# Transposing half of the query tiles on VectorE instead of TensorE, and moving statistics and side sums to other engines, in a fused adaLN block

## The chip, the cores and the metric

The kernel runs on one core of a Trainium2 chip. A core has five engines that each work through a queue of their own, in order, and wait for each other by semaphores: TensorE (PE in the profile, its weight loads PEld), VectorE (DVE), ScalarE (ACT), GpSimd (POOL) and SyncE (SP), which here does nothing but issue DMA transfers. The metric is the device time of one execution in microseconds (us), lower is better.

## The reference

`x` is 2048 tokens of 512 features. Six vectors of modulation come from `silu(c) @ w_mod`. Then, in float32:

```
h = layernorm(x) * (1 + ca) + sa
q, k, v = h @ wqkv                       # 32 heads of 16 features
pq, pk = phi(q), phi(k)                  # phi(t) = (t > 0 ? t + 1 : exp(t)) + 1e-6
o = (pq @ (pk^T v)) / (pq . sum(pk) + 1e-6)        # linear attention, per head
x = x + ga * (o @ wo)
h = layernorm(x) * (1 + cb) + sb
x = x + gb * (((h @ w_gate) * (h @ w_up)) @ w_down)  # 1376 hidden features
```

## The kernel before

The tokens are cut into 16 tiles of 128, four tiles to a chunk (chunks 0 to 3). Float32 products are made of three TensorE products in the type float32r: each operand is split into a high half (a rounded copy, made by ScalarE) and a low half (what is left, made by VectorE or GpSimd), and high x high, high x low and low x high are added up in PSUM (`split` L195, `product` L205).

A first stage computes keys, values and their per-head products for all tiles. From them and `wo` it folds one matrix `wp` per 128 features (`w_out` L596), so that the attention's output of a token tile is its normalised query features times `wp`. The query tiles `phq[i]` are held with tokens in the partitions; `den_a` (L573), `den_b` (L579) and `den_c` (L583) compute each head's denominator and divide by it on VectorE.

The second stage, which the change touches, goes tile by tile. TensorE needs the query tile with features in the partitions, so `turn_a` (L655) transposes it in four 128x128 blocks on TensorE into a PSUM bank; `turn_h` (L661) makes the high half on ScalarE and `turn_l` (L665) the low half on VectorE, both reading the bank. `y_seed` (L680) copies the residual `x` into an accumulator bank on ScalarE, `y_a` (L688) adds the 12 products with `wp` on TensorE, and `y_b` (L697) copies the sum y back to `x` on ScalarE and takes the statistics of the second layer norm on VectorE (`Norm.stats` L225: `bn_stats`, `bn_aggr`). `y_step(i)` (L703) strings this together: transposes of tile i+1, products of tile i, halves of tile i+1, `y_b` of tile i-1, seed of tile i+1. When a chunk's four tiles are done, `rstd_of`, `nmr_of` and `xhat` (L231 to L247) normalise it: VectorE, then one GpSimd power, then VectorE, then four ScalarE passes.

Between the steps of this stage TensorE is fed other work: the last query projections, and, for chunks 0 and 1, the products of three of the eleven blocks of hidden features (`gate_up` L765, `down` L786), whose results VectorE evicts (`evac` L755). The modulated second-norm features of chunks 0 and 1 are also stored to DRAM (`kept`) and loaded back for the last stage. Chunks 2 and 3 are turned for that stage without TensorE: `stow` (L815) writes a tile to DRAM with its 32-row groups regrouped, `unstow` loads it, and `flip` (L827) transposes its 32x32 blocks on VectorE.

The last stage (`ffn` L1091) does the remaining feed-forward products for pairs of chunks, in a form that needs sums and differences of the left operands (`Left.sum` L872: s1 to s4 for two halves, `first[0]` and `first[1]`) and of the right operands (`Right.sums`, `Right.high`, `Right.lows`, L926 to L952).

The order is written out by hand: nothing is reordered, so every engine runs its instructions in the order of the program text from L1136 on. All tiles in SBUF come from one pool of 94 buffers; a new tile takes a free buffer and its first writer waits for that buffer's last readers. All transfers are issued from SP's queue, in order; a transfer that waits holds back those behind it.

Of the kernel before, what the change touches and what calls it, by code (L numbers as in the profile page):

```python
# [24 lines left out]
def tile_adaln_block(  # L25
# [39 lines left out]
    small = pool("small", 2)  # L65
    tiles = pool("tiles", NB)
# [3 lines left out]
    def f32(ap):  # L70
        return ap.bitcast(F32)
# [3 lines left out]
    def T(p, tag, shape=(P, D), dt=F32, bufs=None):  # L75
        cnt[0] += 1
        return p.tile(list(shape), dt, tag="t" if p is tiles else tag, name=f"{tag}_{cnt[0]}", bufs=bufs)

    def B(tag, shape=(P, D), dt=F32):

        return T(tiles, tag, shape, dt)

    def acc_bank():
        return T(ps_acc, "acc")
# [128 lines left out]
    def cut(pair, a, b):  # L213
        return pair[0][:, a:b], pair[1][:, a:b]


    class Norm:
        def __init__(self, tiles):
            self.tiles = tiles
            self.mv = T(small, "mv", (P, NJ, 2))  # L220
            self.n = [None] * NJ
            self.ps = [None] * KD
            self.t = [None] * KD

        def stats(self, *js, of=None):  # L225
            for j in js:
                st = T(small, "st", (P, 6), bufs=4)
                nc.vector.bn_stats(st, self.tiles[j] if of is None else of)
                nc.vector.bn_aggr(self.mv[:, j], st)

        def rstd_of(self, a=0, b=NJ):  # L231
            if a == 0:
                self.rstd = T(small, "rstd", (P, NJ))
                self.nmr = T(small, "nmr", (P, NJ))
                self.ve = T(small, "ve", (P, NJ))
            nc.vector.tensor_scalar(self.ve[:, a:b], self.mv[:, a:b, 1], EPS_LN, None, op0=ALU.add)  # L236
            nc.gpsimd.tensor_tensor(self.rstd[:, a:b], self.ve[:, a:b], half[:, a:b], op=ALU.pow)  # L237

        def nmr_of(self, a=0, b=NJ):
            nc.vector.scalar_tensor_tensor(self.nmr[:, a:b], self.mv[:, a:b, 0], -1.0, self.rstd[:, a:b],  # L240
                                           op0=ALU.mult, op1=ALU.mult)

        def xhat(self, *js):
            for j in js:
# [41 lines left out]
    NT = NCH * NJ  # L286
    norm = [Norm(xts[0])]
    wk, wq, wv = [], [], []
    kx, phk, phq, q_ps = {}, {}, {}, {}
# [169 lines left out]
    rows, cols = {}, {}  # L459
# [113 lines left out]
    def den_a(ch, *js, on=None):  # L573

        for j in js:
            den_p(ch, j, on=on)
            den_r(ch, j)

    def den_b(ch):  # L579
        nc.vector.tensor_tensor(dens[ch], dens[ch], den0.unsqueeze(1).to_broadcast([P, NJ, NH]), op=ALU.add)  # L580
        nc.vector.reciprocal(dens[ch], dens[ch])

    def den_c(*tiles):  # L583

        for i in tiles:
            ch, j = divmod(i, NJ)
            p3 = phq[i].rearrange("p (h i) -> p h i", i=DH)
            nc.vector.scalar_tensor_tensor(p3, p3, EPS_PHI, dens[ch][:, j].unsqueeze(2).to_broadcast([P, NH, DH]),
                                           op0=ALU.add, op1=ALU.mult)
# [65 lines left out]
    def turn_a(i):  # L655
        tps[i] = turn_bank[0]()
        phi = phq.pop(i)
        for k in range(KD):
            nc.tensor.transpose(tps[i][:, k * P:(k + 1) * P], phi[:, k * P:(k + 1) * P], ident)

    def turn_h(i):  # L661
        pqs[i] = (B("xh", dt=F32R), B("xl", dt=F32R))
        nc.scalar.activation(pqs[i][0], tps[i], AF.Copy)

    def turn_l(i):  # L665
        h, l = pqs[i]
        nc.vector.tensor_tensor(l, tps.pop(i), f32(h), op=ALU.subtract)

    def turn(i):
        turn_a(i)  # L670
        turn_h(i)
        turn_l(i)

    y_banks = []

    def y_bank():
# [3 lines left out]
    def y_seed(i, of=acc_bank):  # L680

        yps[i] = of()
        if of is bank:

            nc.tensor.matmul(yps[i], wp[0][0][:, :P], wp[0][0], start=True, stop=True)
        nc.scalar.activation(yps[i], xts[i // NJ][i % NJ], AF.Copy)

    def y_a(i):  # L688
        if i not in yps:
            y_seed(i)  # L690
        pq = pqs.pop(i)
        for k in range(KD):
            (ah, al), (bh, bl) = cut(pq, k * P, (k + 1) * P), wp[k]
            for x, y in ((ah, bh), (ah, bl), (al, bh)):
                nc.tensor.matmul(yps[i], x, y, start=False, stop=k == KD - 1 and x is al, skip_group_check=True)  # L695

    def y_b(i):  # L697
        ch, j = divmod(i, NJ)
        ps = yps.pop(i)
        nc.scalar.activation(xts[ch][j], ps, AF.Copy)  # L700
        norm2[ch].stats(j, of=ps)

    def y_step(i, *more, late=(), q=None, turn=True, seed=acc_bank):  # L703

        if q is not None:
            ps = proj(q, wq)
        if turn and i + 1 < NT and i + 1 not in pqs:
            turn_a(i + 1)
        y_a(i)
        if i + 1 in tps:  # L710
            turn_h(i + 1)
            turn_l(i + 1)
        if i - 1 in yps:
            y_b(i - 1)
        if q is not None:
            q_a(q, ps)
        if seed and i + 1 < NT:
            y_seed(i + 1, seed)
        for do in more:
            do()  # L720
        for do in late:
            do()
# [14 lines left out]
    def scale_down(f):  # L737
        d = raw_f[f][2]
        nc.vector.tensor_tensor(d, d, gb[:d.shape[0]], op=ALU.mult)
# [46 lines left out]
    def down(ch, js=range(NJ), ahead={}, parts=(lone,)):  # L786

        dn = {j: acc_bank() for j in js}
        for step, (part, j) in enumerate((part, j) for part in parts for j in js):
            for do in ahead.get(step, ()):  # L790
                do()
            a, b = j * P, (j + 1) * P
            for f in part:
                n = fts[f][1]
                (hh, hl), (dh, dl) = hs[ch, f], wf[f][2]
                nc.tensor.matmul(dn[j], hh[:n, a:b], dh[:n], start=f == lone[0], stop=False)
                nc.tensor.matmul(dn[j], hh[:n, a:b], dl[:n], start=False, stop=False)
                nc.tensor.matmul(dn[j], hl[:n, a:b], dh[:n], start=False, stop=f == lone[-1])
        return lambda: evac(ch, dn, js)
# [15 lines left out]
    def stow(ch, *js):  # L815

        for j in js:
            to = stowed[ch, j] = tc.dram_tile([P, D], F32, name=f"stowed_{ch}_{j}")
            to = to.rearrange("(q i) (m c) -> m i q c", i=BL, c=P)
            for m in range(NQ):  # L820
                nc.sync.dma_start(to[m], norm2[ch].n[j][m * BL:(m + 1) * BL].rearrange("i (q c) -> i q c", c=P))
# [37 lines left out]
    class Left:  # L859
# [9 lines left out]
                c, k = self.of[n]  # L869
                self.f[n] = load(kept[c][k], "f") if c in PLAIN else blocks.pop((c, "f", k))  # L870

        def sum(self, *names):  # L872
            for n in names:
                x, y, alu = {"s1": ("a21", "a22", ALU.add), "s3": ("a11", "a21", ALU.subtract),
                             "s2": ("s1", "a11", ALU.subtract), "s4": ("a12", "s2", ALU.subtract)}[n]
                self.f[n] = B("s")
                nc.vector.tensor_tensor(self.f[n], self.f[x], self.f[y], op=alu)

        def split(self, *names, low=None):
            for n in names:  # L880
# [265 lines left out]
    y_step(0, lambda: den_c(3), lambda: q_b(11))  # L1146
    y_step(1)
    y_step(2, lambda: split_gu(f0, nc.gpsimd))
    y_step(3, lambda: scale_down(f0), turn=False, seed=False)
    ps12 = proj(12, wq)  # L1150
    y_b(3)
    norm2[0].rstd_of()
# [36 lines left out]
    den_c(7)  # L1189
    den_a(2, 2, on=nc.vector)  # L1190
    g()
    y_step(5)
    y_step(6, lambda: den_a(2, 3, on=nc.vector))
    y_step(7, turn=False, seed=False)
    y_b(7)
    norm2[1].rstd_of()
    den_b(2)
    ln2_nx(1)
    den_c(8)
    take = down(0, ahead={3: (lambda: turn(8), lambda: y_seed(8, bank), lambda: den_c(9, 10))})  # L1200
    take()
    ln2_turn(1, 0, 1)
    y_step(8)
    ln2_turn(1, 2, 3)
    y_step(9)
    side.update(plain_side((0, 1)))
    first = [Left((0, 1), k).into(side) for k in range(KH)]
    for x in first:
# [2 lines left out]
    right_load(1)  # L1211
    g = gate_up(1, f0)
    den_a(3, 0, 1, on=nc.vector)
    den_c(11)
    g()
    y_step(10)
    g = gate_up(1, f1)
    den_a(3, 2, 3, on=nc.vector)
    g()
    y_step(11, turn=False, seed=False)  # L1220
    y_b(11)
    norm2[2].rstd_of()
    den_b(3)
    g = gate_up(1, f2)
    den_c(12)
    norm2[2].nmr_of()
    norm2[2].xhat(0, 1)
    first[0].sum("s1", "s3")
    g()
    norm2[2].xhat(2, 3)  # L1230
    stow(2, 0, 1, 2, 3)
    turn_a(12)
    take = down(1, (0, 1), parts=((f0, f1), (f2,)))
    den_c(13)
    turn_h(12)
    turn_l(12)
    y_banks += [acc_bank(), acc_bank()]
    y_seed(12, y_bank)
    first[0].sum("s2", "s4")
    take()  # L1240
    den_c(14)
    y_step(12, seed=y_bank)
    take = down(1, (2, 3))
    first[1].sum("s1", "s3", "s2", "s4")
    first[0].split("s1", "s2")
    take()
    den_c(15)
    y_step(13, seed=y_bank)
    right_sums(0, nc.vector)
    for n in range(4):  # L1250
        banks.append(bank())
# [88 lines left out]
```

## Time and profile before

| | |
|---|---|
| median of 3 runs | 561.06 us (560.93 to 561.57) |
| the profiled execution | 560.93 us, span of its trace 559.2 us |
| granted TensorE clock | 0.999 |
| statistics of y, VectorE L228 | 690 ns each |
| transposes of query tiles, TensorE L659 | 64 |
| DMA, all of the span | 52.01 MB, 29.1% of the 16 engines |

The span is what the trace covers; the time of the execution is 1.7 us longer. A row of a group gives line, engine, operation, output <- input, shape, count, then busy time in us and mean ns of one, then the idle time of the engine before them and what ended it. In the chain that ended last each row is a start, a length and the work that held the end up at that moment. In a row of a table by stage stand the stage, then for PE, PEld, DVE, ACT and POOL the busy us with the count of instructions, then the granted clock, the DMA share and GB/s.

### The profile page before, as it was taken

To read this page: it belongs to the slowest core of one execution; us is meant where nothing else is said; L and a number is where in the kernel's file an instruction comes from. 1 tells how busy PE (TensorE), PEld (TensorE's weight loads), DVE (VectorE), ACT (ScalarE), POOL (GpSimd) and SP (SyncE) were. 2 spreads that over 40 slices of the span, in tenths; PEclk is the share of its full clock that TensorE was granted. 3 is DMA by queue.
4 is the path that set the end of the run, shared out by engine and by line. 5 is a ranking of instruction groups with operands and counts; after the bars stand their busy time and mean duration, and the time that the engine had idled before them with its cause. 6 is when DMAs were issued, how large, how long until landed. Compare 5 with 4: busy or idle time off the path is not lost.

```text
span 559.2 us, 7301 instructions
## 1 busy us (share of the span) xinstructions
PE 552.8 (99%) x2539; PEld 453.4 (81%) x2539; DVE 383.7 (69%) x629; ACT 281.0 (50%) x503; POOL 190.1 (34%) x195
## 2 busy tenths in 40 slices
PE   8999999999999999999999999999999999999997
PEld 6788888888888778878887888877888888888886
DVE  7896968968969876859877697796543544344435
ACT  3695866546557546344883445554343333333110
POOL 2000000100011300001599666566667446446200
PEclk9999999999999999999999999999999999999999
DMA  8900212210501000814425152591335222200004
GB/s 289 385 4 2 75 55 96 93 60 3 154 2 74 2 1 38 264 33 119 132 59 149 58 192 71 175 321 36 114 113 151 56 57 57 58 19 1 1 0 151
DMA packets 51077, 52.01 MB, mean 93 GB/s; under 512 B 7712, under 2 KB 32544, under 8 KB 51040
## 3 DMA queue, kind: packets, MB, share of 16 engines
q1 hardware_dynamic: 51040, 51.54, 29.1%
q8 instruction: 20, 0.33, 0.2%
q14 instruction: 17, 0.14, 0.1%
HBM read 39.46 MB, written 12.06 MB: 92 GB/s over the span
## 4 chain that ended last, share of the span: by engine, by line
PE 88%; DVE 5%; ACT 2%; DMA 1%; issue 1%; POOL 1%; SPq 1%; POOLq 0%; ACTq 0%; DVEq 0%
PE bank L959 28%; PE acc L1039 6%; PE acc L1041 6%; PE acc L1040 6%; PE acc L695 5%; PE bank L209 5%; PE bank L211 5%; PE bank L210 5%; PE acc L338 3%; PE acc L337 3%; PE acc L336 3%; PE bank L772 2%; PE bank L774 2%; PE bank L773 2%; PE bank L259 2%
## 5 line engine op out<-in xcount | busy, mean ns | idle before, releaser
L959 PE MATMUL bank<-h,w 128*128 128x512 f32 (+1 forms) x798 | 185.1, 390 | 0.2 <-DVE u L1018 0.2
L959 PEld LDWEIGHTS bank<-h,w 128*128 128x128 f32 (+1 forms) x798 | 148.2, 186 | 34.0 <-DVE u L1018 1.0
L964 ACT ACTIVATE bank<-bank 128x512 f32<-128x512 f32 (+1 forms) x38 | 22.1, 583 | 135.2 <-PE bank L959 135.2
L759 DVE TENSOR_TENSOR x<-acc,x 128x512 f32<-128x512 f32 (+1 forms) x73 | 48.5, 682 | 47.4 <-PE acc L1041 47.4
L945 POOL TENSOR_TENSOR w<-raw,w 128x256 fp32r<-128x256 f32 (+3 forms) x38 | 41.9, 1101 | 107.8 <-ACT w L938 107.8
L1039 PE MATMUL acc<-w,kh 128*128 128x512 f32 (+2 forms) x154 | 59.6, 387 | 0.0
L1040 PE MATMUL acc<-w,kh 128*128 128x512 f32 (+2 forms) x154 | 59.6, 387 | 0.0
L1041 PE MATMUL acc<-w,kl 128*128 128x512 f32 (+2 forms) x154 | 59.5, 386 | 0.0
L197 POOL TENSOR_TENSOR w<-raw,w 128x512 fp32r<-128x512 f32 (+1 forms) x25 | 35.4, 1421 | 54.3 <-ACT w L196 54.3
L237 POOL TENSOR_TENSOR rstd<-ve,half 128x4 f32<-128x4 f32 (+1 forms) x10 | 10.6, 1061 | 122.8 <-DVE ve L236 121.1
L945 POOL TENSOR_TENSOR w<-t,w 128x512 fp32r<-128x512 f32 (+1 forms) x38 | 48.5, 1296 | 0.0
L197 DVE TENSOR_TENSOR kl<-u,kh 128x512 fp32r<-128x512 f32 (+1 forms) x38 | 26.7, 743 | 29.9 <-ACT kh L196 29.9
L209 PE MATMUL bank<-w,h 128*128 128x512 f32 x104 | 40.8, 392 | 0.0
L211 PE MATMUL bank<-w,h 128*128 128x512 f32 x104 | 40.5, 390 | 0.0
L210 PE MATMUL bank<-w,h 128*128 128x512 f32 x104 | 40.5, 389 | 0.0
L695 PE MATMUL acc<-w,xh 128*128 128x512 f32 x120 | 38.2, 400 | 0.0
L1039 PEld LDWEIGHTS acc<-w,kh 128*128 128x128 f32 (+1 forms) x154 | 28.9, 188 | 6.0
L1040 PEld LDWEIGHTS acc<-w,kh 128*128 128x128 f32 (+1 forms) x154 | 28.9, 188 | 6.0
L1041 PEld LDWEIGHTS acc<-w,kl 128*128 128x128 f32 (+1 forms) x154 | 28.9, 188 | 5.9
L1018 DVE TENSOR_TENSOR u<-bank,u 128x512 f32<-128x512 f32 (+1 forms) x19 | 13.1, 688 | 27.5 <-PE bank L959 20.7
L246 ACT ACTIVATE n<-x,nmr,rstd 128x512 f32<-128x512 f32 x30 | 22.9, 804 | 16.3 <-DVE nmr L240 15.0
L196 ACT ACTIVATE w<-raw 128x512 fp32r<-128x512 f32 (+2 forms) x44 | 26.3, 618 | 2.0 <-DMA raw<-in_A_wqkv_dram 1.1
(198 smaller groups left out, 1112.9 us busy)
## 6 DMA issues: line engine op xcount, KB each, us to landing
raw<-in_w_mod_dram SPq DMA_DIRECT2D x24, 256.0 KB, 3.7
raw<-in_B_w_down_dram SPq DMA_DIRECT2D x20, 256.0 KB, 2.9
raw<-in_B_w_gate_dram SPq DMA_DIRECT2D x36, 128.0 KB, 3.5
raw<-in_B_w_up_dram SPq DMA_DIRECT2D x36, 128.0 KB, 3.6
x<-in_A_x_dram SPq DMA_DIRECT2D x16, 256.0 KB, 5.4
out_dram<-x SPq DMA_DIRECT2D x15, 256.0 KB, 2.7
raw<-in_A_wqkv_dram SPq DMA_DIRECT2D x12, 256.0 KB, 5.3
kept<-f SPq DMA_DIRECT2D x8, 256.0 KB, 2.0
```

The lines of the kernel that those rows point to most:

```text
L196: nc.scalar.activation(h, src, AF.Copy)
L197: (low or nc.vector).tensor_tensor(l, src, f32(h), op=ALU.subtract)
L209: nc.tensor.matmul(ps, ah, bh, start=i == 0, stop=False)
L210: nc.tensor.matmul(ps, ah, bl, start=False, stop=False)
L211: nc.tensor.matmul(ps, al, bh, start=False, stop=i == n - 1)
L695: nc.tensor.matmul(yps[i], x, y, start=False, stop=k == KD - 1 and x is al, skip_group_check=True)
L759: nc.vector.tensor_tensor(xt[:, a:b], dn[j][:, a:b], xt[:, a:b], op=ALU.add)
L945: sub = lambda out, x, y: (on or nc.gpsimd).tensor_tensor(out, x, f32(y), op=ALU.subtract)
L959: mm = lambda x, y, **kw: nc.tensor.matmul(ps, x[:, k], y, skip_group_check=True, **kw)
L1039: nc.tensor.matmul(ps, hh[:, a:b], dh[:n, c:d], start=i == 0, stop=False)
L1040: nc.tensor.matmul(ps, hh[:, a:b], dl[:n, c:d], start=False, stop=False)
L1041: nc.tensor.matmul(ps, hl[:, a:b], dh[:n, c:d], start=False, stop=i == len(hs) - 1)
```

## The change

Query tiles 8 to 15 (9 to 16 counted from one) are no longer transposed by TensorE. Once divided (`den_c`), a tile is stored to DRAM (`move_out`), loaded back by four transfers that put the 128-feature groups into 32 partitions each (`move_in`), and transposed in 32x32 blocks by VectorE into an SBUF tile (`turn_v`), from which the halves are made as before. The features then stand in the partitions in another order, four apart; so a second copy of `wp`, with its rows in that order, is made by storing it to DRAM (`wp_store`, 8 transfers) and loading it back (`wp_fetch`, 8), and the products of these tiles use it.

For chunks 0 to 2 the statistics of y are taken by ScalarE (`stats_act`): the copy to `x` also gives the sum over the features, and a second pass, in place in PSUM, gives the sum of the squared differences. Chunk 3 keeps `bn_stats`.

The eight sums of `first[0]` and `first[1]` go to GpSimd. The divisions and the denominators of chunks 2 and 3 stand earlier, and `stow(2, ...)` stands later, behind the loads of tiles 14 and 15.

```diff
+        def stats_act(self, j, of):
+            if j == 0:
+                self.sums = T(small, "sums", (P, 2, NJ))
+            out = self.tiles[j]
+            nc.scalar.activation(out, of, AF.Copy, accum_out=self.sums[:, 0, j:j + 1])
+            nc.scalar.activation(of, of, AF.Square, scale=-float(D), bias=self.sums[:, 0, j:j + 1],
+                                 accum_out=self.sums[:, 1, j:j + 1])
...
+    FLIPPED = range(8, NT)
+    SUMS = (0, 1, 2)
+    def wp_store():
+        to = [tc.dram_tile([D, D], F32, name=f"wp_{part}") for part in range(2)]
+        for g in range(KD):
+            for part in range(2):
+                nc.sync.dma_start(to[part][g * P:(g + 1) * P], f32(wp[g][part]))
+        wp4.append(to)
+    def wp_fetch():
+        rows = [x.rearrange("(p k) d -> p k d", k=KD) for x in wp4.pop()]
+        for k in range(KD):
+            wp4.append((B("w", dt=F32R), B("w", dt=F32R)))
+            for part in range(2):
+                nc.sync.dma_start(f32(wp4[k][part]), rows[part][:, k])
+    def move_out(*tiles):
+        for i in tiles:
+            moved[i] = tc.dram_tile([P, D], F32, name=f"moved_{i}")
+            nc.sync.dma_start(moved[i], phq.pop(i))
+    def move_in(*tiles):
+        for i in tiles:
+            v = moved[i].rearrange("(m i) (q c) -> q i m c", i=BL, c=P)
+            moved[i] = B("u")
+            for q in range(NQ):
+                nc.sync.dma_start(moved[i][q * BL:(q + 1) * BL].rearrange("i (m c) -> i m c", c=P), v[q])
+    def turn_v(i):
+        tps[i] = B("f")
+        nc.vector.transpose(tps[i].rearrange("p (s m i) -> p m s i", m=NQ, i=BL),
+                            moved.pop(i).rearrange("p (m i s) -> p m s i", m=NQ, i=BL))
+    def turned_v(i):
+        turn_v(i)
+        turn_h(i)
+        turn_l(i)
+    def ready(*tiles):
+        den_c(*tiles)
+        move_out(*tiles)
...
-            (ah, al), (bh, bl) = cut(pq, k * P, (k + 1) * P), wp[k]
+            (ah, al), (bh, bl) = cut(pq, k * P, (k + 1) * P), (wp4 if i in FLIPPED else wp)[k]
...
+        if ch in SUMS:
+            norm2[ch].stats_act(j, ps)
+            return
         nc.scalar.activation(xts[ch][j], ps, AF.Copy)
         norm2[ch].stats(j, of=ps)
...
-        if turn and i + 1 < NT and i + 1 not in pqs:
+        if turn and i + 1 < NT and i + 1 not in pqs and i + 1 not in FLIPPED:
...
-                nc.vector.tensor_tensor(self.f[n], self.f[x], self.f[y], op=alu)
+                (on or nc.vector).tensor_tensor(self.f[n], self.f[x], self.f[y], op=alu)
...
-    y_step(3, lambda: scale_down(f0), turn=False, seed=False)
+    y_step(3, lambda: scale_down(f0), wp_store, turn=False, seed=False)
...
-    y_step(5)
-    y_step(6, lambda: den_a(2, 3, on=nc.vector))
-    y_step(7, turn=False, seed=False)
+    y_step(5, lambda: den_a(2, 3, on=nc.vector), wp_fetch)
+    y_step(6, lambda: den_b(2), lambda: ready(8))
+    y_step(7, lambda: ready(9), lambda: move_in(8), turn=False, seed=False)
     y_b(7)
     norm2[1].rstd_of()
-    den_b(2)
+    ready(10)
     ln2_nx(1)
-    den_c(8)
-    take = down(0, ahead={3: (lambda: turn(8), lambda: y_seed(8, bank), lambda: den_c(9, 10))})
+    take = down(0, ahead={1: (lambda: move_in(9), lambda: ready(11)),
+                          3: (lambda: turned_v(8), lambda: y_seed(8, bank), lambda: move_in(10, 11), lambda: turn_v(9))})
     take()
     ln2_turn(1, 0, 1)
-    y_step(8)
+    y_step(8, lambda: turn_v(10))
     ln2_turn(1, 2, 3)
-    y_step(9)
+    y_step(9, lambda: turn_v(11))
...
     g = gate_up(1, f1)
     den_a(3, 2, 3, on=nc.vector)
+    den_b(3)
+    ready(12, 13)
     g()
-    y_step(11, turn=False, seed=False)
+    y_step(11, lambda: move_in(12), turn=False, seed=False)
     y_b(11)
     norm2[2].rstd_of()
-    den_b(3)
     g = gate_up(1, f2)
-    den_c(12)
+    ready(14, 15)
+    move_in(13)
     norm2[2].nmr_of()
     norm2[2].xhat(0, 1)
-    first[0].sum("s1", "s3")
+    first[0].sum("s1", "s3", on=nc.gpsimd)
     g()
     norm2[2].xhat(2, 3)
-    stow(2, 0, 1, 2, 3)
-    turn_a(12)
+    turn_v(12)
     take = down(1, (0, 1), parts=((f0, f1), (f2,)))
-    den_c(13)
     turn_h(12)
     turn_l(12)
+    move_in(14, 15)
+    stow(2, 0, 1, 2, 3)
     y_banks += [acc_bank(), acc_bank()]
     y_seed(12, y_bank)
-    first[0].sum("s2", "s4")
+    first[0].sum("s2", "s4", on=nc.gpsimd)
     take()
-    den_c(14)
-    y_step(12, seed=y_bank)
+    turn_v(13)
+    y_step(12, lambda: turn_v(14), seed=y_bank)
     take = down(1, (2, 3))
-    first[1].sum("s1", "s3", "s2", "s4")
+    first[1].sum("s1", "s3", "s2", "s4", on=nc.gpsimd)
     first[0].split("s1", "s2")
     take()
-    den_c(15)
-    y_step(13, seed=y_bank)
+    y_step(13, lambda: turn_v(15), seed=y_bank)
```

More of the change, by code (lines that the diff above doesn't have):

```diff
@@ L222, in __init__ @@
             self.ps = [None] * KD
+            self.sums = None
             self.t = [None] * KD
@@ L235, in rstd_of @@
                 self.ve = T(small, "ve", (P, NJ))
-            nc.vector.tensor_scalar(self.ve[:, a:b], self.mv[:, a:b, 1], EPS_LN, None, op0=ALU.add)
+            if self.sums is not None:
+                nc.vector.tensor_scalar(self.ve[:, a:b], self.sums[:, 1, a:b], float(D) ** -3, EPS_LN, op0=ALU.mult, op1=ALU.add)
+            else:
+                nc.vector.tensor_scalar(self.ve[:, a:b], self.mv[:, a:b, 1], EPS_LN, None, op0=ALU.add)
             nc.gpsimd.tensor_tensor(self.rstd[:, a:b], self.ve[:, a:b], half[:, a:b], op=ALU.pow)
         def nmr_of(self, a=0, b=NJ):
-            nc.vector.scalar_tensor_tensor(self.nmr[:, a:b], self.mv[:, a:b, 0], -1.0, self.rstd[:, a:b],
-                                           op0=ALU.mult, op1=ALU.mult)
+            mean, by = (self.mv[:, a:b, 0], -1.0) if self.sums is None else (self.sums[:, 0, a:b], -1.0 / D)
+            nc.vector.scalar_tensor_tensor(self.nmr[:, a:b], mean, by, self.rstd[:, a:b], op0=ALU.mult, op1=ALU.mult)
         def xhat(self, *js):
@@ L672, in turn @@
         turn_l(i)
+    FLIPPED = range(8, NT)
+    SUMS = (0, 1, 2)
+    wp4, moved = [], {}
+    def wp_store():
[31 more added lines that the diff above has]
+        move_out(*tiles)
     y_banks = []
@@ L870, in get, with sum @@
                 self.f[n] = load(kept[c][k], "f") if c in PLAIN else blocks.pop((c, "f", k))
-        def sum(self, *names):
+        def sum(self, *names, on=None):
             for n in names:
@@ L1213, in tile_adaln_block @@
     den_a(3, 0, 1, on=nc.vector)
-    den_c(11)
     g()
```

## The prediction

> **What bounds the kernel now.** I read the page first, then the chain that ended last, then the waits of TensorE.
>
> ```profile
> span 559.2 us, 7301 instructions
> PE 552.8 (99%) x2539; PEld 453.4 (81%) x2539; DVE 383.7 (69%) x629; ACT 281.0 (50%) x503; POOL 190.1 (34%) x195
> PE 88%; DVE 5%; ACT 2%; DMA 1%; issue 1%; POOL 1%; SPq 1%; POOLq 0%; ACTq 0%; DVEq 0%
> ```
>
> ```profile
> PE bank L959 <- DVE u L1018: 0.2, 1, 0.2
> ```
>
> TensorE is busy 99% of the span and owns 88% of the chain; behind the first loads the last line is its only wait above 0.1 us. It is the bound: time is won only by taking instructions from it, and lost wherever it is made to wait. The other 12% of the chain lies mostly in one stretch, from 247 to 297 us, which the chain walks through without TensorE:
>
> ```profile
> 247.23 0.80 ACT n L246
> ...
> 291.61 2.85 DVE kl L197 x2
> ...
> 296.35 0.69 DVE u L1018
> 297.08 1.65 PE bank L959 x6
> ```
>
> At 297 TensorE waited 0.2 us for VectorE. So in this stretch VectorE, ScalarE and GpSimd are just as late as TensorE, and a TensorE that arrives sooner finds them not ready unless their own work shrinks too. That is the question of this change.
>
> **The gain.** Tiles 8 to 15 lose their four transposes each on TensorE (L659). The chain gives the price in place, from start to start:
>
> ```profile
> L659 PE MATMUL bank<-ident,h x60: 270/272/273, 150.9 to 260.3; 128*128 128x128 f32 x60
> ```
>
> ```profile
> 184.75 0.44 PE bank L659 x4
> ```
>
> One transpose lasts 0.27 us, but they are pipelined, and four take 0.44 us of the queue. Eight tiles: 8 x 0.44 = **3.5 us**. Nothing else leaves TensorE.
>
> **Off the path.** Per tile VectorE gains one 32x32-block transpose, and for chunks 0 to 2 loses the statistics, while ScalarE gains a Square pass. Eight side sums go from VectorE to GpSimd.
>
> ```profile
> L829 DVE STREAM_TRANSPOSE wide<-u x8: 1050/1082/1132, 294.4 to 338.1; 128x512 f32<-128x512 f32 x8
> L228 DVE BATCH_NORM_STATS2 st<-acc 128x6 f32<-128x512 f32 x15 | 10.3, 690 | 4.4 <-ACT x L700 4.4
> L327 ACT ACTIVATE kh<-phi,eps_phi 128x512 fp32r<-128x512 f32 x16 | 11.5, 718 | 5.7 <-DVE phi L304 4.9 <-PE bank L210 0.7
> L877 DVE TENSOR_TENSOR s<-f,f x8: 683/686/1777, 246.4 to 363.6; 128x512 f32<-128x512 f32 x8
> L945 POOL TENSOR_TENSOR w<-t,w 128x512 fp32r<-128x512 f32 x36 | 46.5, 1311 | 0.0
> ```
>
> VectorE: 8 x 1.08 = 8.7 us more; 12 x 0.69 = 8.3 (with their small aggregates) and 8 x 0.69 = 5.5 less. ScalarE: 12 x 0.72 = 8.6 us more, taking the row with a bias held per partition. GpSimd: 8 x 1.3 = 10.4 us more, from about 244 us on, where it was idle. In sum all three fit; what counts is where each stands in its queue.
>
> **DMA.** The round trip adds 16 transfers for the weights and, per tile, one store of 256 KB and four loads of 64 KB, all issued from the one SP queue in order. The weights' trip is issued behind the load of sb4 (160.83 below) and needed at 218: nothing. For a tile:
>
> ```profile
> kept<-f SPq DMA_DIRECT2D x8, 256.0 KB, 2.0
> stowed<-n SPq DMA_DIRECT2D x32, 64.0 KB, 1.8
> cb_row<-col SPq DMA_DIRECT2D x1, 2.0 KB, 8.4
> ```
>
> ```profile
> 160.83 0.33 SPq L812 DMA_DIRECT2D sb<-sb_row  x1
> 247.35 7.65 SPq L821 DMA_DIRECT2D stowed<-n  x16
> 268.17 3.00 SPq L115 DMA_DIRECT2D u<-stowed  x4
> 203.94 0.69 DVE L667 TENSOR_TENSOR xl<-bank,xh 128x512 fp32r<-128x512 f32 x1 [0.71 <-ACT xh L663]
> 210.84 0.95 DVE L581 RECIPROCAL den<-den 128x128 f32<-128x128 f32 x1
> 218.78 0.71 PE L695 MATMUL bank<-w,xh 128*128 128x512 f32 x2
> 221.61 0.68 DVE L667 TENSOR_TENSOR xl<-bank,xh 128x512 fp32r<-128x512 f32 x1
> 223.40 0.39 PE L695 MATMUL acc<-w,xl 128*128 128x512 f32 x1
> ```
>
> Tile 8: the low half of tile 7 ends at 204.6, the den step (0.3 + 0.95) and the scaling (0.68) follow at once, 206.5; issue 0.48 (16 issues in 7.65) and landing 2.0, 209.0; four issues 1.9 and landing 1.8 (a load was not seen in this form; the stow moves the same 512-byte pieces the other way), 212.7; transpose 1.08 and halves 0.6 + 0.7, 215.1. TensorE wants it at 218.78 - 2 x 0.44 = 217.9. Hidden, with 2.8 us of cover; a landing as long as the longest row, 8.4 us (4-byte pieces), would cost 3.8 here. Queued behind the waiting transpose on VectorE are tile 9's transpose and the four evictions of `down(0)`; those are ready at 217 and lose nothing. Tile 9 is the next late one: its low half ended at 222.3 for a use at 223.4, and TensorE gains 1.3 us on it while ScalarE's modulation before it gains 0.4; cover about 0.2 us, cost 0. For tiles 12 to 15 the scaling moves ahead of 244 us and the trips have about 4 us of cover; stow(2), now behind them in SP's queue, is read back only at 268 us.
>
> **Term A, the Square ahead of the seed.** ScalarE is in order, and in `y_step` the seed of the next accumulator now stands behind a copy and a Square.
>
> ```profile
> 162.10 0.61 ACT L686 ACTIVATE acc<-x 128x512 f32<-128x512 f32 x1
> 163.71 0.61 PE L695 MATMUL acc<-w,xh 128*128 128x512 f32 x2
> 201.94 0.59 ACT L686 ACTIVATE acc<-x 128x512 f32<-128x512 f32 x1
> 203.27 5.50 PE acc L695 x24
> ```
>
> Tile 3 has 163.71 - 162.71 = 1.0 us of cover and tile 6 has 203.27 - 202.53 = 0.74. The Square takes 0.72 and some 0.1 of overlap that its wait for the sum undoes: tile 3 keeps 0.2, tile 6 loses 0.1. No row shows what the accumulating output costs: from nothing to a pass of its own (the reduction, 0.69) on each of the two. I take 0.1 each, nearest to the plain rows: A = 0.3 us over tiles 3, 6 and 7; ends 0.1 and 1.0 for small prices, more for the rival below.
>
> **Term B, tile 12.** Its transpose stands on VectorE behind the low half of the last `gate_up(1, f2)`.
>
> ```profile
> 247.79 0.39 PE L774 MATMUL bank<-h,w 128*96 128x512 f32 x1
> 249.93 0.69 DVE L197 TENSOR_TENSOR kl<-phi,kh 96x512 fp32r<-96x512 f32 x1 [0.70 <-ACT kh L196]
> 252.98 0.71 PE L695 MATMUL acc<-w,xh 128*128 128x512 f32 x2
> 264.02 0.88 POOL L945 TENSOR_TENSOR w<-raw,w 128x256 fp32r<-128x256 f32 x1 [18.38 <-ACT w L938]
> 281.86 1.85 DVE L197 TENSOR_TENSOR kl<-u,kh 128x512 fp32r<-128x512 f32 x2
> 280.00:290.00 10.00, 10.00 (x46) 8.29 (x45) 8.07 (x13) 8.58 (x16) 9.92 (x10) 1.00 0.19 50
> ```
>
> Four tiles earlier (1.8 us) the products end at 248.18 - 1.8 = 246.4. Product, high and low half (at most 0.69 each, and hand-overs) end at 248.5, the transpose at 249.6, the high half on ScalarE at 250.2, seed and low half at 250.7 and 250.9. TensorE, six tiles ahead, wants the high half and the seed at 252.98 - 2.64 = 250.3: a wait of 0.4 us that the kernel before, whose TensorE transposes tile 12 without waiting for VectorE, does not have. But GpSimd, idle there before (the 18.38 us in its row), now runs its sums, and beside a GpSimd that is 99% busy VectorE's two-input operations on SBUF took 1.85/2 and 2.85/2 us instead of 0.69, on average 0.49 more. Two such stand in this path, and the new low half is one only because its source moves from PSUM to SBUF: the low half ends at 251.9 for a use at 250.8. B = **1.1 us**; ends 0.4 (no collision) and 1.5 (both as the dearer pair).
>
> The Trainium skill's page "SBUF — State Buffer", section "SBUF: two separate sides", says that the pair shared by VectorE and GpSimd is an exclusive lock held for the whole instruction, and that the loser blocks. The pairs above agree in direction; they are shorter than a full block each time. It speaks against moving the sums here; its outcome is a rival below.
>
> **Term C, the stretch to 297.**
>
> ```profile
> 259.88 1.28 DVE L759 TENSOR_TENSOR x<-acc,x 128x512 f32<-128x512 f32 x2
> 263.10 0.41 DVE L927 TENSOR_TENSOR t<-raw 128x256 f32<-128x256 f32 x1
> ```
>
> VectorE loses the sums (5.5 us) and four scalings (2.4) before 263 us and gains four transposes (4.3), but the evictions at 259.88 still follow TensorE. From them, two evictions, a low half, the statistics and tile 15's transpose lead to the sums of the first right side at 261.7 instead of 263.1: 1.4 us earlier. TensorE comes 3.5 - A - B = 2.1 earlier. From there ScalarE, VectorE and GpSimd are full to 297, so TensorE is given back to their lead: C = 0.3, since part of that lead was TensorE's own wait of 0.2 and the sums on VectorE no longer meet GpSimd; ends 0 and 0.7.
>
> **Sum.** 3.5 - 0.3 - 1.1 - 0.3 = 1.8 us. The profiled execution took 560.93 us (span 559.2 and 1.7 around it); the median of the runs is 561.06, 0.13 more. Forecast 559.13 + 0.1 = **559.2 us**.
>
> **Rivals.**
> *All hidden.* VectorE and GpSimd miss each other and the freed VectorE time covers tile 12: terms 0 to 0.5 in all, 557.9. For it: VectorE's balance is -5 us. Against: the 0.4 us of B needs no collision. Chance 0.20.
> *Full block.* Each of the two operations of B waits out a whole GpSimd operation, 1.3 us: the low half ends at 253.5, B = 2.7, time 560.8: no difference. This is the mechanism of the lock as the page above has it. The transposes, several of them beside a busy GpSimd, kept 1.05 to 1.13 us, so it would strike only these two. Chance 0.16.
> *Slower: the accumulating output is a pass of its own.* If ScalarE pays 0.69 us for each of the two sums, a tile's copy and Square cost 1.4 more, and seeds come late by 1.2 us at tile 3, 1.5 at tile 6 and as much at tile 7 behind it: 4.2 instead of 0.3, 563.1. It decides from about 1.1 us per tile, where these three waits eat the 1.8 us and 0.2% more. For it: no row shows such an output. Against: VectorE's statistics form two moments in one pass of 0.69. Chance 0.20; I count here, at like size, the round trip that lands in 8.4 us.
> *Forecast.* The rest, 0.44.
>
> **How the numbers follow.** A measurement of this kernel can tell about 0.2% (1.1 us) from no change. Faster by more: all of the first rival and four fifths of the forecast, 0.20 + 0.35 = 0.55. Within: the full block and the rest of the forecast, 0.16 + 0.09 = 0.25. Slower: 0.20. The forecast's own range, by the ends of A, B and C (0.5 to 3.2 given back), is 558.0 to 560.7. The range given goes from 557.4, just under the first rival, to 562.4, and leaves out most of the slower case.
>
> **What would show it.** No L659 past tile 7, TensorE's instructions down by 32. At the products of tile 12 a TensorE wait for the low half of about 1 us, with GpSimd's L940 beside VectorE operations of over 1 us; no wait at tiles 8 to 11. At tiles 6 and 7 waits for the seed of 0.3 us or less. ScalarE's Square near 0.72 us. It is wrong if TensorE waits for a transposed tile's loads, if the Square pair costs over 2 us, or if the wait near 297 has grown beyond 1 us.

## The result, and the profile after

The changed kernel takes 562.58 us (median of 22 runs, 560.79 to 564.03), the kernel before 561.26 (22 runs, 560.62 to 562.35). The ratio is 1.0019, 95% interval 1.0010 to 1.0027: slower by about 1.1 us (1.3 between the medians), where the prediction had 559.2 and a gain of 1.9. First the page of the changed kernel, its three lines that answer to those of before:

```profile
span 561.0 us, 7363 instructions
PE 553.5 (99%) x2507; PEld 452.0 (81%) x2507; DVE 379.2 (68%) x605; ACT 291.4 (52%) x539; POOL 201.1 (36%) x203
PE 84%; DVE 7%; ACT 4%; issue 2%; DMA 2%; POOL 1%; SPq 0%; ACTq 0%; POOLq 0%; DVEq 0%
```

TensorE has 32 instructions fewer, as it should, and is busy 0.7 us longer. Its share of the chain fell from 88% to 84%. Next the waits of TensorE that the change brought or moved (engine, line, what it waited for: us in total, times, longest):

```profile
PE acc L755 <- ACT acc L746: 1.2, 2, 1.0
PE bank L1022 <- DVE u L1081: 0.2, 1, 0.2
PE acc L861 <- DVE kl L197: 0.2, 1, 0.2
```

The seed (L746) is waited for twice: 0.24 us at tile 6 and 0.97 at tile 12. TensorE's timeline around tile 12, with start and length in us:

```profile
250.51 0.50 PE L861 MATMUL acc<-w,kl 96*128 96x512 f32 x1 [0.21 <-DVE kl L197]
...
251.31 0.40 PE L861 MATMUL acc<-w,kl 96*128 96x512 f32 x1
252.68 0.76 PE L755 MATMUL acc<-w,xh 128*128 128x512 f32 x2 [0.97 <-ACT acc L746]
253.44 0.80 PE L755 MATMUL acc<-w,xl 128*128 128x512 f32 x1
```

The first product of tile 12 starts 1.37 us after the one ahead of it, where products follow each other every 0.23 us: 1.14 lost. Counted in the same way, from start to start, the product at 250.51 loses 0.37 where the list shows a wait of 0.21 (the one ahead of it started at 249.91), and tile 6 loses 0.50 where it shows 0.24 (its products start 0.85 us after the transposes ahead of them, 0.35 in the kernel before). And the product at 253.44 takes 0.80 us, where L755 takes 0.39. The table by stage, cut at the moments at which the clock changes, says why:

```profile
249.84:253.25 3.41, 2.23 (x8) 1.00 (x7) 2.71 (x3) 2.16 (x4) 3.41 (x4) 1.00 0.58 146
253.25:256.66 3.41, 3.40 (x9) 2.55 (x9) 2.71 (x5) 1.01 (x2) 2.55 (x2) 0.50 0.55 135
```

In the 3.41 us up to 253.25 TensorE was busy for 2.23; in the next 3.41 us the granted clock is 0.50, and nine products are done in the time of fifteen. By the clock, half of 3.41, 1.7 us, is lost on top of the wait; the spans below say 1.5. Now VectorE, ScalarE and GpSimd ahead of that product:

```profile
244.78 1.26 DVE L254 SCALAR_TENSOR_TENSOR nmr<-sums,rstd 128x4 f32<-128x4 f32 x1 [0.30 <-POOL rstd L250]
...
249.50 0.95 DVE L197 TENSOR_TENSOR kl<-phi,kh 96x512 fp32r<-96x512 f32 x1 [0.70 <-ACT kh L196]
250.37 1.10 DVE L722 STREAM_TRANSPOSE f<-u 128x512 f32<-128x512 f32 x1
252.17 1.22 DVE L680 TENSOR_TENSOR xl<-f,xh 128x512 fp32r<-128x512 f32 x1 [0.70 <-ACT xh L676]
```

```profile
246.08 1.52 ACT L259 ACTIVATE n<-x,nmr,rstd 128x512 f32<-128x512 f32 x2 [2.98 <-DVE nmr L254]
247.50 0.58 ACT L843 ACTIVATE phi<-bank 96x512 f32<-96x512 f32 x1
...
251.50 0.63 ACT L676 ACTIVATE xh<-f 128x512 fp32r<-128x512 f32 x1 [0.62 <-DVE f L722]
252.04 0.58 ACT L746 ACTIVATE acc<-x 128x512 f32<-128x512 f32 x1
```

```profile
244.73 2.55 POOL L940 TENSOR_TENSOR s<-f,f 128x512 f32<-128x512 f32 x2
```

In the kernel before, two of the operations that will matter have their usual length on VectorE:

```profile
245.71 0.69 DVE L588 SCALAR_TENSOR_TENSOR h<-h,den 128x512 f32<-128x512 f32 x1
246.32 0.15 DVE L240 SCALAR_TENSOR_TENSOR nmr<-mv,rstd 128x4 f32<-128x4 f32 x1
```

The seed reads only `x` and was long possible, but on ScalarE it stands behind the high half, which waits for tile 12's transpose on VectorE, which stands behind the low half of `gate_up(1, f2)`. That low half is late because `nmr`, an operation on 4 columns, took 1.26 us instead of 0.15: it started 0.05 us after the first of the two side sums on GpSimd and ended about when that ended (246.0). So the two xhat passes (L259), which need it, start late on ScalarE, and `phi` (L843), which the low half is made of, stands behind them. The low half itself takes 0.95 instead of 0.69 beside a later side sum. What follows on VectorE 11 us later:

```profile
261.62 0.69 DVE L822 TENSOR_TENSOR x<-acc,x 128x512 f32<-128x512 f32 x1 [1.37 <-PE acc L861]
262.23 0.68 DVE L680 TENSOR_TENSOR xl<-f,xh 128x512 fp32r<-128x512 f32 x1
262.83 0.69 DVE L229 BATCH_NORM_STATS2 st<-acc 128x6 f32<-128x512 f32 x1
263.56 0.18 DVE L230 BATCH_NORM_AGGREGATE mv<-st 128x2 f32<-128x6 f32 x1
263.74 1.10 DVE L722 STREAM_TRANSPOSE f<-u 128x512 f32<-128x512 f32 x1
264.76 0.83 DVE L990 TENSOR_TENSOR t<-raw 128x256 f32<-128x256 f32 x1
```

The last eviction waits 1.37 us for the late TensorE, and tile 15's transpose stands ahead of the first right sum (L990, `t<-raw`). That sum starts at 264.76 us; in the kernel before (L927) at 263.10. It will turn out to be the row to watch.

Each execution comes with its granted clock. Of the 22 of the changed kernel, 8 have 0.998 or more ("full clock" below), with a median span of 559.55 us; 14 have less, with 561.05. The 79 executions of the kernel before beside the experiments: 46 at full clock, 559.3; 33 below, 560.1. So at full clock the change wins nothing (+0.25). In these runs the clock is below full more often with it (14 of 22 against 33 of 79, a difference that so few runs do not settle), and that costs more (1.5 us against 0.8). Only the profiled execution shows where the clock fell; for the other 13 the place is not shown.

### The profile page after: what moved, and what is told of

It reads as the page before. It is cut to its first block, busy times and chain, and to the rows that moved or that the text cites. A ratio compares the mean times of both kernels' runs of the same rounds, so it can differ in the third digit from the quotient of the medians.

```text
span 561.0 us, 7363 instructions
## 1 busy us (share of the span) xinstructions
PE 553.5 (99%) x2507; PEld 452.0 (81%) x2507; DVE 379.2 (68%) x605; ACT 291.4 (52%) x539; POOL 201.1 (36%) x203
## 4 chain that ended last, share of the span: by engine, by line
PE 84%; DVE 7%; ACT 4%; issue 2%; DMA 2%; POOL 1%; SPq 0%; ACTq 0%; POOLq 0%; DVEq 0%
PE bank L1022 28%; PE acc L1102 6%; PE acc L1103 6%; PE acc L1104 6%; PE acc L755 5%; PE bank L209 5%; PE bank L211 5%; PE bank L210 5%; PE acc L351 3%; PE acc L349 3%; PE acc L350 3%; PE acc L148 2%; PE bank L272 1%; DMA w<-wp 1%; PE acc L859 1%
## 5 line engine op out<-in xcount | busy, mean ns | idle before, releaser
L755 PE MATMUL acc<-w,xh 128*128 128x512 f32 x120 | 38.9, 406 | 1.2 <-ACT acc L746 1.2
L259 ACT ACTIVATE n<-x,nmr,rstd 128x512 f32<-128x512 f32 x30 | 22.9, 804 | 15.6 <-DVE nmr L254 15.6
L755 PEld LDWEIGHTS acc<-w,xh 128*128 128x128 f32 x120 | 22.5, 194 | 6.6 <-ACT acc L746 2.3
```

What stands on the lines that cost most here:

```text
L259: nc.scalar.activation(self.n[j], self.tiles[j], AF.Identity, scale=self.rstd[:, j:j + 1], bias=self.nmr[:, j:j + 1])
```

## The theories

**M**: the order at tile 12 makes TensorE wait; the wait lowers its clock; from about 260 us the evictions, VectorE's queue and the first right sum hand the delay on to the end. **S**: ScalarE's longer statistics are the loss. **G**: GpSimd's sums, which hold VectorE up, are the loss. **C**: from 260 to 297 us VectorE, ScalarE and GpSimd set the pace whatever TensorE does.

## The experiments

The times stand beside the kernel before on the same chip (561.1 to 561.5 us). "Start" is that of the first right sum in the profiled execution, "rest" its span less the start.

| kernel | us | ratio (95%) | span at full clock | below full clock | start | rest |
|---|---|---|---|---|---|---|
| before | | | 559.3 | 33 of 79 | 263.10 | 296.1 |
| changed | 562.58 | 1.0019 (1.0010 to 1.0027) | 559.55 | 14 of 22 | 264.76 | 296.2 |
| e1, tile 12 forward | 559.62 | 0.9971 (0.9960 to 0.9982) | 557.9 | 0 of 7 | 261.72 | 296.2 |
| e2, gap filled | 561.58 | 1.0007 (0.9996 to 1.0018) | 559.6 | 2 of 11 | 263.54 | 296.3 |
| e3, sums on VectorE | 563.40 | 1.0043 (1.0028 to 1.0057) | 561.1 | 5 of 8 | 264.85 | 296.2 |
| e4, statistics on VectorE | 561.64 | 1.0001 (0.9989 to 1.0012) | 559.0 | 7 of 11 | 262.93 | 296.2 |
| e5, no transposes | 559.38 | 0.9968 (0.9956 to 0.9980) | 557.7 | 0 of 5 | 261.41 | 296.2 |
| e6, e1 + e4 | 559.59 | 0.9970 (0.9961 to 0.9979) | 557.5 | 2 of 9 | 262.04 | 296.2 |
| e7, e1 + sums at 230 us | 563.16 | 1.0032 (1.0020 to 1.0043) | 559.25 | 9 of 11 | 265.00 | 296.1 |
| e8, e1 + tile 15 later | 558.63 | 0.9959 (0.9946 to 0.9972) | 556.8 | 1 of 5 | 260.64 | 296.1 |
| e9, before + GpSimd sums | 562.79 | 1.0033 (1.0020 to 1.0046) | 561.1 | 0 of 5 | 264.70 | 296.2 |
| e10, e8 + chunk 1 on VectorE | 558.20 | 0.9949 (0.9937 to 0.9961) | 556.3 | 1 of 5 | 260.78 | 296.1 |
| e11, tile 15 later alone | 561.58 | 1.0004 (0.9990 to 1.0018) | 558.1 | 7 of 12 | 262.25 | 296.1 |
| e12, e10 + sums on VectorE | 560.19 | 0.9976 (0.9967 to 0.9985) | 557.95 | 5 of 11 | 262.72 | 296.1 |

The last column is the main finding: in all fourteen profiled executions the end comes 296.05 to 296.26 us after VectorE starts the first right sum, however TensorE stands at that moment. In e1 and e8, for one, TensorE starts the products of tile 14 at the same time (261.56 and 261.59), and the spans are 557.9 and 556.7.

**e1, tile 12 forward.** Its transpose goes ahead of the eviction of the last `gate_up`, its high half and seed ahead of two xhat passes.

```diff
     first[0].sum("s1", "s3", on=nc.gpsimd)
+    turn_v(12)
     g()
-    norm2[2].xhat(2, 3)
-    turn_v(12)
     take = down(1, (0, 1), parts=((f0, f1), (f2,)))
     turn_h(12)
-    turn_l(12)
-    move_in(14, 15)
-    stow(2, 0, 1, 2, 3)
     y_banks += [acc_bank(), acc_bank()]
     y_seed(12, y_bank)
+    turn_l(12)
+    norm2[2].xhat(2, 3)
+    move_in(14, 15)
+    stow(2, 0, 1, 2, 3)
```

> The changed kernel with the work for tile 12 moved forward: its transpose on VectorE stands ahead of the eviction of the last gate_up, its high half and its seed on ScalarE ahead of the last two xhat passes. Theory M (a wait at tile 12 and what follows from it): in the changed kernel TensorE stands still for 1.2 us before the products of tile 12 (0.97 of it put down to the seed), and then runs 3.41 us at half clock, which costs 1.7 more. Here the wait is under 0.3 us, the granted clock is 1.00 in every run, and the time is 560.3 (559.8 to 561.2), below the kernel before by 0.5 to 1.5 us. Rival S (the statistics on ScalarE are the loss) and rival C (VectorE's queue up to 297 us is the loss, TensorE's wait is hidden behind it): the wait goes, the time stays at 562 or more. Rival G (GpSimd's sums hold VectorE up): the low half of tile 12 is still late, about 562.

559.62, at full clock in all seven runs. Its TensorE and VectorE rows:

```profile
251.52 0.63 PE L755 MATMUL acc<-w,xh 128*128 128x512 f32 x2
```

```profile
261.72 0.83 DVE L990 TENSOR_TENSOR t<-raw 128x256 f32<-128x256 f32 x1
```

Tile 12 starts at 251.52 without a wait (252.68 before), the right sum 3.0 us earlier than in the changed kernel. The time lies 0.2 below theory M's range, on M's side; S, C and G, which had 562, fall as explanations of the whole.

**e2, the gap filled.**

```diff
     turn_v(13)
+    for _ in range(5):
+        nc.tensor.matmul(y_banks[1], wp[0][0][:, :P], wp[0][0], start=True, stop=True)
     y_step(12, lambda: turn_v(14), seed=y_bank)
```

> The changed kernel with five idle products (1.14 us) on TensorE between down(1, (0, 1)) and tile 12, into a bank that nothing reads, so that TensorE works where it waited. Theory M: the products of tile 12 start at the same moment as in the changed kernel, but the clock stays at 1.00 in every run; the half-clock stretch of 3.41 us is gone and with it 1.7 us: span near 559.5, time 561.2 (560.8 to 561.8), equal to the kernel before. If the lower clock costs nothing (rival C: the stretch up to 297 us is held by other engines), or if the clock does not depend on the wait: 562.5, clock 0.996.

```profile
251.77 1.32 PE L1307 MATMUL acc<-w 128*128 128x512 f32 x5
252.93 0.70 PE L755 MATMUL acc<-w,xh 128*128 128x512 f32 x2
```

Tile 12 is as late as in the changed kernel, but the half clock is gone from this profile; 2 runs of 11 are below full clock instead of 14 of 22. The time falls by 1.0 us (0.7 by the ratios, whose intervals overlap a little) to that of the kernel before (561.58, ratio 1.0007). At full clock nothing is won (559.6 against 559.55): what the idle products save is the half clock alone. That the two runs fell nevertheless is not explained: there is no trace of them.

**e3 and e4, one part each back on VectorE.** The side sums (`on=nc.gpsimd` taken out three times), and the statistics (`SUMS = ()`).

> The changed kernel with the eight side sums back on VectorE. Theory M: nmr loses its 1.1 us stretch beside GpSimd and the low half of tile 12 its 0.5, but VectorE has 0.7 us per sum more in its queue; the wait at tile 12 shrinks from 1.2 to 0.6 to 1.0, the clock still falls in part of the runs, time 561.5 to 562.8. Rival G (GpSimd's sums are the loss): wait gone, 560.5 or less.

> The changed kernel with the statistics of chunks 0 to 2 back on VectorE (bn_stats), so that ScalarE pays 0.58 us for y and not 1.65. Theory M: the waits at tiles 6 and 7 (0.24 us) go, the one at tile 12 stays (the seed still stands behind the high half), time 562.2 (561.5 to 562.8). Rival S (the statistics on ScalarE are the loss): 560.7 or less.

e3 is slower still, 563.40, outside of both expectations: VectorE, with 5.5 us more to do, now comes late at tile 14, where TensorE waits 2.6 us:

```profile
264.31 1.22 PE L755 MATMUL acc<-w,xh 128*128 128x512 f32 x2 [2.58 <-ACT acc L746]
```

So G fails in this kernel: it needs GpSimd's help. But the same run shows whose work makes most of the wait at tile 12: without GpSimd's sums `nmr` takes 0.17, the low half of `gate_up(1, f2)` ends at 249.17 instead of 250.45, the 0.21 at L861 is gone and the wait at tile 12 is 0.28 instead of 0.97, less than theory M had. The sums on GpSimd cost there and win more ahead of tile 14. e4 lies in the lower part of M's range (561.64); the wait at tile 6 is gone, the one at tile 12 is there (0.98 in its profile, without a half clock that time). S fails too, having asked for 560.7.

**e5, the transposes left out of the kernel before.**

```diff
     def turn_a(i):
+        if i >= 8:
+            tps[i] = phq.pop(i)
+            return
```

> The kernel before with the four TensorE transposes of tiles 8 to 15 left out and nothing put in their place: the halves are made of the tile as it stands, not turned, so 3.5 us leave TensorE and no other engine gains or loses an operation (the attention of these tiles is not the reference's). It asks what the freed TensorE time is worth at the end. Rival T (TensorE sets the end throughout): all of it, 557.8 against 561.3 before. Theory M with term C (from 260 to 297 us VectorE, ScalarE and GpSimd hold TensorE up, and only the 2 to 2.5 us by which their start follows TensorE come through): 559.2 (558.6 to 559.8). Rival C (that stretch does not follow TensorE at all): 560.9 or more.

```profile
261.97 0.72 PE L698 MATMUL acc<-w,xh 128*128 128x512 f32 x2 [1.04 <-ACT acc L689]
```

559.38, as M with term C had it: of 3.5 us only 1.6 come through at full clock (spans 559.3 and 557.7), 1.8 between the medians of all runs, in which the kernel before has its half clocks. A TensorE that arrives sooner waits 1.04 us for the seed of tile 14, which waits for VectorE's statistics. So even transposes that cost nothing win only about the 1.8 us that the forecast had left after its three terms. To win more, VectorE's queue has to shrink as well: e10, below, wins 3.0 at full clock.

**e6, e7, e8, starting from e1.** Statistics on VectorE; the sums issued at 230 us; and tile 15 later:

```diff
-    y_step(13, lambda: turn_v(15), seed=y_bank)
+    y_step(13, seed=y_bank)
     right_sums(0, nc.vector)
+    turn_v(15)
```

> The kernel with tile 12 moved forward (559.62, ratio 0.9971 to before), and the statistics of chunks 0 to 2 back on VectorE. It asks whether ScalarE's statistics win or lose anything once tile 12 no longer waits. Theory M: the 0.24 us wait at tile 6 goes, nothing else: 559.4 (559.1 to 559.9). Rival S (ScalarE's longer y stage costs): 558.9 or less. If VectorE needs the relief: 560.2 or more.

> The kernel with tile 12 moved forward, and the eight side sums issued on GpSimd as soon as their loads are there (from about 230 us, where GpSimd has nothing to do until 243) instead of beside nmr and the low halves of 245 to 256 us. If GpSimd beside VectorE costs on the path: nmr is back at 0.2 us from 1.26, the low half of the last gate_up at 0.69 from 0.95, TensorE's 0.2 us wait for it goes, and the evictions start that much earlier: 559.2 (558.8 to 559.5). If the lengthened operations all had room: 559.6. If the sums now hold up VectorE's work of 230 to 242 us: 560 or more.

> The kernel with tile 12 moved forward, and tile 15's transpose on VectorE behind the sums of the first right side instead of ahead of them. If VectorE's queue sets the start of the stretch up to 297 us (term C): those sums start 1.1 us earlier (260.7 instead of 261.7 in the profile), and the time falls by 0.5 to 1.1 to 558.8 (558.5 to 559.2), unless tile 15 is then late at 270 us. If TensorE or the loads of the right sides set it: 559.6.

e6 equals e1 within the noise, in theory M's range; at full clock it is 0.4 shorter. Its profiled execution has the clock low elsewhere, in the first stage, which all these kernels share:

```profile
15.00:20.00 5.00, 5.00 (x18) 3.95 (x18) 4.23 (x11) 4.98 (x9) 0.00 (x0) 0.66 1.05 404
```

That costs 0.7 us (558.2 against 557.5). In the profiles of e10 and e12 the clock is halved at the same place. It is likely what the 33 executions of the kernel before show at the like price of 0.8, but there is no trace of those.

e7 failed, 563.16: on GpSimd's idle time the sums met VectorE's denominators instead.

```profile
234.95 1.77 DVE L578 TENSOR_TENSOR f<-h,zb 128x512 f32<-128x512 f32 x1
```

```profile
251.47 0.50 PE L859 MATMUL acc<-w,kh 96*128 96x512 f32 x1 [1.65 <-ACT kh L196]
```

L578 takes 0.65 alone, and 1.61 and 1.77 here; the delay ran through the statistics of chunk 2 to a 1.65 us wait, and the clock fell in 9 of 11 runs. Idle time of GpSimd is not free where VectorE is busy.

e8 is the clear hit of term C, 558.63:

```profile
260.64 0.39 DVE L990 TENSOR_TENSOR t<-raw 128x256 f32<-128x256 f32 x1
...
262.64 1.11 DVE L722 STREAM_TRANSPOSE f<-u 128x512 f32<-128x512 f32 x1
```

The transpose steps behind the sums, these start 1.1 us sooner, and the end follows by 1.1.

**e9, e10, e11, e12.** The kernel before with GpSimd's sums alone; e8 with `SUMS = (0, 2)`; the changed kernel with tile 15 later alone; e10 with the sums on VectorE.

> The kernel before with nothing changed but the eight side sums on GpSimd. It asks whether what was won with tiles 12 and 15 reordered (558.63) is the freed TensorE time or only the relief of VectorE. Theory M (in the kernel before the evictions at 259.88 us follow TensorE, so a lighter VectorE changes nothing there): 561.2 (560.7 to 561.7), the kernel before. Rival V (VectorE's load is what the reordered kernel won): 559.5 to 560.3.

> The kernel with tile 12 moved forward and tile 15's transpose put behind the right sums (558.63, ratio 0.9959 to before), and the statistics of chunk 1 alone back on VectorE, so that the seed of tile 6 is no longer late. If TensorE is now the bound again from 196 us to the end: the 0.27 us wait is won, 558.4 (558.1 to 558.6). If the stretch up to 297 us still takes such gains: 558.6.

> The changed kernel with tile 15's transpose behind the right sums, tile 12 as it was. TensorE's wait at tile 12 and the half clock behind it remain. If VectorE's queue holds the stretch back by itself, its 1.1 us come on top whatever tile 12 does: 561.5 (561.1 to 562.0), with the clock at 0.996 in part of the runs. If the late evictions (the wait) set the stretch and the transpose has room behind them: 562.5.

> The fastest arrangement so far (tile 12 forward, tile 15's transpose behind the right sums, chunk 1's statistics on VectorE: 558.20) with the eight side sums back on VectorE. On the kernel before, moving these sums to GpSimd cost 1.7 us, since GpSimd held up a scaling and nmr on VectorE. If that is what they do here too, VectorE alone is better: 557.5 or less. If here, with the scalings moved ahead of them, the 5.5 us that they take off VectorE between 245 and 262 us count for more than the collisions: 559.0 or more, with TensorE waiting for a seed near 260 us as in the run with the sums back on VectorE.

e9 refutes both expectations: 562.79, slower by 0.33% at full clock. Rows of VectorE, and GpSimd's:

```profile
245.46 1.75 DVE L588 SCALAR_TENSOR_TENSOR h<-h,den 128x512 f32<-128x512 f32 x1
247.14 1.25 DVE L240 SCALAR_TENSOR_TENSOR nmr<-mv,rstd 128x4 f32<-128x4 f32 x1
```

```profile
245.37 3.00 POOL L877 TENSOR_TENSOR s<-f,f 128x512 f32<-128x512 f32 x2
```

Alone these two take 0.69 and 0.15. Each starts just after a GpSimd sum and is 1.1 us longer, about what was left of that sum; the xhat passes come 1.9 us later, and TensorE waits three times (0.7, 0.2, 0.5). This is the lock of the Trainium skill's page "SBUF — State Buffer", section "SBUF: two separate sides", by which the loser waits out the whole operation: for these two the trace agrees. In the changed kernel the transposes beside GpSimd's sums kept 1.10 to 1.12, and the low half at 249.50 grew by 0.26 where 0.4 of a sum was left.

e10 is the fastest, 558.20, 0.5% below the kernel before and in the range of its first expectation. e11 shows that tile 15 counts without tile 12 too: 561.58 as expected, 1.45 at full clock, with half clocks in 7 of 12 runs. e12, with the sums on VectorE, is 1.65 us slower than e10 at full clock, as its second expectation had it, and has tile 14's wait again:

```profile
263.27 0.73 PE L755 MATMUL acc<-w,xh 128*128 128x512 f32 x2 [1.35 <-ACT acc L746]
```

The sums on GpSimd lose 1.8 us of span at full clock in the kernel before and win 1.65 in e10, where the scalings stand ahead of them and `nmr` (1.25) and two low halves (0.95 and 1.14) are hit, but no scaling.

## Why the prediction was wrong

The direction was wrong, and three steps failed: term B was too small and went by another path, term C was too small, and a price for the clock was missing. None of the three signs of error that the text named came: no transposed tile's load was waited for, copy and Square with their two accumulator reads cost 1.6 us, and the wait near 297 is 0.25.

**The gain**: right as far as it goes. 32 instructions and their 3.5 us left TensorE, and nothing else did. What the 3.5 are worth at the end belongs to term C.

**DMA**: right. The four loads landed in 2.0 us (median), tiles 8 to 11 never waited.

**Term A** (0.3): the kind was right, the size 0.5, within its ends. Square takes 0.66; the accumulating output is an instruction of its own on ScalarE, 0.19 where 0.1 was taken:

```profile
L237 ACT ACTIVATE x<-acc x11: 577/595/599, 158.6 to 241.6; 128x512 f32<-128x512 f32 x11
L237 ACT ACTIVATION_READ_ACCUMULATOR x<-acc x11: 189/194/208, 159.0 to 242.1; 128x1 f32 x11
L238 ACT ACTIVATE acc<-acc,sums x11: 662/662/662, 159.3 to 242.3; 128x512 f32<-128x512 f32 x11
```

From start to start tile 6 lost 0.50, and no other tile ahead of tile 12 waited for its seed; undoing it for that chunk won 0.5 (e8 to e10, spans at full clock). The rival of a whole pass per sum is out.

**Term B** (1.1; ends 0.4 and 1.5): the place was right, the size 1.65 (span at full clock, changed kernel to e1), outside of its ends. The path was another: not the low half but the seed. The text has the seed behind the high half (250.7, the 0.4 us), but adds the collisions to the low half alone, although the first of them moves the transpose, the high half and the seed too. And GpSimd's sums struck one step ahead of where they were priced as well, at `nmr`, for the whole of what was left of a sum: the mechanism of the rival "full block", at an instruction that the text left out, since alone it takes 0.15. That it counts is shown by e3, where this low half ends 1.28 us earlier. The two collisions that the text did price at 0.49 each came too, at 0.26 and 0.53.

**The clock**: the step that is missing. Every wait was priced at its own length. Here a wait of 1.1 us had a second price: 3.41 us at half clock in the profiled execution, and 14 of 22 runs below full clock, with a span 1.5 us longer. By the spans at full clock (+0.25) the result without it would have been "no difference"; none of the rivals had it. The Trainium skill's page "TensorE: Matmul & The Clock Gate", Part 1, has the length of the window, 3413 ns, with which the 3.41 agrees; its rule that the clock falls after an idle window does not cover this trace, where a window busy for 2.23 of 3.41 us came before it. The traces also show in part why the same wait lowers the clock in one execution and not in another. Every change of the clock inside a span falls on a step of 3.413 us, counted from the first change that the trace records. Cut so, the step with the long wait was busy for 0.89 (e3), 1.76 (e7) and 2.23 us (changed kernel) where the clock fell behind it, and for 2.25 (e4), 2.37 (e5), 2.42 (e12) and 2.45 (e11) where it did not: it matters how a wait falls across two steps. This orders these seven executions and is no threshold, for in the first stage the clock fell behind steps that count as busy for 3.3 us and more (e6, e10, e12).

**Term C** (0.3; ends 0 and 0.7): mis-sized. In e5, which has neither A nor B, 1.9 of the 3.5 us are held back, with VectorE's queue as in the kernel before. The prediction forecast the first right sum 1.4 us earlier, TensorE 2.1 earlier, and yet let 1.8 come through; the table's last column says that only the sum's start counts, so its own rows gave 1.4. In the changed kernel that sum was 1.66 later instead of 1.4 earlier, since the evictions ahead of it follow a TensorE that had waited and run slow; e1, without the wait, has 261.72 to the forecast's 261.7. And tile 15's transpose, which the text counted in that queue, cost 1.1 to 1.45 of span that moving one line gave back.

**The ledger**, in spans at full clock: 559.3 less 3.5 would be 555.8. The changed kernel has 559.55. Of the 3.75 given back, 1.65 is tile 12 (to e1), 1.1 tile 15 (to e8), 0.5 tile 6 (to e10); 0.5 is left at 556.3, of which 0.37 is the wait at L861 counted from start to start, and the rest is open. The prediction had 1.7 given back: 0.3 for tile 6 and its like, 1.1 for tile 12, 0.3 for the stretch with tile 15. The half clocks come on top.

## What to carry to other kernels

Look for the instruction whose start the end follows at a fixed distance; here VectorE's first right sum, and neither TensorE's 99% nor its own waits would name it. Where an operation on the bound engine is given to another, check what the operations behind it in each in-order queue wait for, above all a cheap one (a seed) behind one that waits. And price a wait of a busy TensorE of about a microsecond at more than its length: here the clock could fall behind it.

## What the runs showed of the hardware

An accumulating output on ScalarE costs a separate 0.19 us each time. An operation on 4 columns on VectorE, beside a GpSimd sum, grew from 0.15 to 1.26 us, and a scaling of 512 columns from 0.69 to 1.75; 32x32-block transposes of 512 columns stayed at 1.08 to 1.12. TensorE ran 3.41 us at half clock after a stretch in which it stood still for 1.2 of 3.41 us; the same wait did so in some executions and not in others (after 2.23 us busy in a step of 3.413, but not after 2.25).
